# Two small products of each chunk alternate in one TensorE call, and the hand-written order of a recurrence and gated MLP kernel is rewritten

## The chip, the cores and the metric

The kernel runs on one core of one Trainium2 chip. The metric is device time in microseconds (us) of one execution. The inputs are laid out on the host before the launch; all arithmetic is on the chip. Three timed runs and one profiled run of the kernel before are at hand.

## The reference

A recurrence over 768 time steps (4 batches, 8 heads, head size 40) is followed by a gated MLP over its output. Cut to what matters:

```python
for t in range(S):                                   # S = 768, state: B x H x 40 x 40
    y[:, :, t] = einsum('bhd,bhde->bhe', r_t, state)
    Sa = einsum('bhde,bhe->bhd', state, a_t)
    state = state * w_t[:, :, None, :] - einsum('bhd,bhe->bhde', Sa, b_t)
    state = state + einsum('bhd,bhe->bhde', v_t, k_t)
x = y with the heads side by side                    # B x S x 320
h = maximum(x @ w_in, 0); u, v = halves of h         # 512 columns each
v_n = (v - mean(v)) / sqrt(var(v) + 1e-6)
gated = u * (w_spatial @ v_n + b_spatial)
out = gated @ w_out
```

## The kernel before, in words

The recurrence is worked in chunks of 64 time steps. There are 24 chunks: 12 in time for each of two pairs of batches. In a chunk the 16 heads of a pair lie as 8 units on the columns and 2 parities on the partitions (0 to 63 and 64 to 127). The recurrence inside a chunk becomes a triangular system, so that a chunk is a sequence of small fp32 products. TensorE runs each fp32 product as two instructions, so that a call with 16 products is 32 instructions in a trace.

The first phase (function `phase1`) has five kinds of calls; a call is a short function that issues one step of one chunk.

- Preparation: `prep_load` fetches the early inputs (tile `ein`), `scan1` and `scan2` are the two running products on VectorE, `at_mul` and `sl_mul` scale the inputs by them (tiles `at`, `sl`). `lprime` is the triangular block on TensorE and `lblock` masks it into tile `Lc`. Four chunks at a time are inverted on VectorE in 33 steps (`invert`, lines L636 to L663, most of the steps being the pair L652 and L656).
- Products of a chunk that don't need the state. `b_lka` (L790) multiplies the keys `sl` by `at` into a PSUM tile `bk`, and `b_lka_out` copies the two halves on ScalarE (L807) and masks them on GpSimd (L797). `b_h` (L820) multiplies the two halves of the late inputs (tile `lin`) into another `bk`, and `b_h_out` copies (L830) and masks it likewise. `b_tok` (L842), `b_l21` (L859), `b_zt` (L879) and `b_x21` (L907) are smaller ones. All of them, and `lprime`, take their PSUM from one pool with two banks, `bk`.
- The chain through the state: `c_bp` (L943), `c_bp_out` on ScalarE (L952), `c_ff` (L960), `c_ff_out` (L968), `c_xx` (L981), `c_xx_out` (L992), `c_mp` (L1005, L1011), `c_mp_out` on VectorE (L1025 or L1028 and L1029), which gives the state (tile `Mc`) of the next chunk's `c_bp`; and `c_y` (L1039), `c_y_out` (L1053), which give the chunk's output. `c_bp` and `c_xx` of a chunk are already written so that two groups alternate product by product.
- The MLP's first half on blocks of 128 steps whose chunks are done: `m_load`, `m_split`, `m_u` (L1160), `m_v` (L1114) and the normalisation `m_n1`, `m_root`, `m_n2`, `m_n3`. Their PSUM is one bank, `pv`; before the first block that bank is idle.
- `dec`: six decodings of the 64-bit input weights on VectorE, nine steps each.

Each engine takes its instructions in program order. That order is a table written out by hand: `SCHED` gives each call a place on an axis of about one unit per chunk, the calls are sorted by place (`plan.sort()`), and those below 24 are issued in exactly that order. The order on SyncE's queue, which issues nearly all DMAs, comes from the same table. Calls from 24 on and the second phase are ordered by the tile framework's scheduler. The second phase (`phase2`) is the spatial product (L423), the gate (L429) and the output projection (L478). Its weights are prepared during the first phase by `wprep` (three generators of 13 steps: one DMA, four differences L337, eight casts and differences L350 and L348) and four decodings of 9 steps. A second table, `W_PLAN`, gives a place on the same axis to each of these steps; the step is put behind the instruction that stands at that place. The first spatial product needs the weights of all three generators.

Of the kernel before, what the change touches and what calls it, by code (L numbers as in the profile page):

```python
# [8 lines left out]
F32 = mybir.dt.float32  # L9
# [25 lines left out]
    "at_mul": (-27657, -25313, -23639, -18952, -9411, 2307, 12016, 21892, 22896, 33609, 48172, 63070,  # L35
        75123, 78303, 98223, 107429, 122495, 124169, 145260, 160660,),
    "b_copy": (-29498, -29163, -16943, -7737, -5728, -5561, 7663, 7831, 17037, 17205, 30596, 31600, 39970,
# [19 lines left out]
    "b_tok": (-26987, -28828, -12759, 3813, 298, 2139, 14192, 8333, 28085, 23733, 43151, 42314, 55538,  # L57
# [3 lines left out]
    "b_tok_out": (-26150, -28493, -12591, 4483, 465, 2809, 16200, 9170, 28253, 25909, 43485, 43820, 55705,  # L61
# [3 lines left out]
    "b_w": (-24643, -20793, -16274, -25648,),  # L65
    "b_w_out": (-24309, -20626, -16106, -25480,),
# [1357 lines left out]
```

## Time and profile before

| | us |
|---|---|
| median of three runs | 670.09 (668.71 to 677.4) |
| the profiled execution, its own time | 670.43 |
| its span, first to last instruction | 668.5 |
| TensorE matmul busy | 564.6 (84%) |
| VectorE busy | 529.1 (79%) |
| ScalarE busy | 419.3 (63%) |
| GpSimd busy | 216.3 (32%) |

Busy time is the time in which an engine has at least one instruction running, so that overlapping matmuls count once. The span has three kinds of stretches, seen in the table of windows: a start, in which every engine waits at times; the chunks, in which TensorE and VectorE both work most of the time; and the second phase, in which TensorE hardly stops. An engine's idle time matters only where the next link of the chain waits for that engine.

### The profile page before, as it was taken

Reading aid. Unit: us, or ns where it says so; the run is one execution under the profiler, and the core shown is the slowest. Engines: PE = TensorE matmul, PEld = TensorE weight load, DVE = VectorE, ACT = ScalarE, POOL = GpSimd, SP = SyncE. Lnnn points to the kernel's source line nnn. Section 1 sums busy time; section 2 is a strip of 40 time slices with the busy share of each in tenths; the row PEclk is TensorE's granted clock in tenths of the full one; section 3 lists DMA queues with packets and bytes.
Section 4 is the critical chain, followed back from the end, with each engine's and each line's share of the span. In section 5 each row is a group of like instructions: output and inputs, shape, how many; then the busy total and the mean of one; then the engine's idle time right before and its main releaser. Section 6 shows DMA issues by size and latency. Waiting matters only on the chain.

```text
span 668.5 us, 27225 instructions
## 1 busy us (share of the span) xinstructions
PE 564.6 (84%) x11504; PEld 498.1 (75%) x11504; DVE 529.1 (79%) x1111; ACT 419.3 (63%) x934; POOL 216.3 (32%) x290
## 2 busy tenths in 40 slices
PE   1657778868768787997999898997998999999997
PEld 1546667656656676786888786886887899999997
DVE  7885369898999899997999679866859987776752
ACT  3344556676757788876888687795975654434422
POOL 5201122143544465522433333240424300522221
PEclk9965877899898999998999889896999999999999
DMA  8375523157466464455554553344346755444111
GB/s 191 62 146 98 120 41 93 38 133 132 80 146 141 104 122 98 106 125 126 157 128 114 146 151 107 104 116 134 102 131 195 232 179 164 138 126 139 58 50 59
DMA packets 116169, 80.79 MB, mean 121 GB/s; under 512 B 45648, under 2 KB 108368, under 8 KB 114448
## 3 DMA queue, kind: packets, MB, share of 16 engines
q1 hardware_dynamic: 115504, 77.35, 46.8%
q10 hardware_dynamic: 544, 1.72, 1.2%
q8 instruction: 90, 1.47, 1.0%
q14 instruction: 31, 0.25, 0.2%
HBM read 58.52 MB, written 20.50 MB: 118 GB/s over the span
## 4 chain that ended last, share of the span: by engine, by line
PE 48%; DVE 26%; DMA 9%; issue 6%; ACT 5%; SPq 5%; DVEq 0%; ACTq 0%
PE pg L423 12%; PE po L478 6%; DMA ein<-in_early 5%; DVE itmp L652 4%; PE pv L1114 4%; PE pv L1160 4%; PE ch L960 3%; DVE A L656 3%; PE bp L943 2%; PE bp L1039 2%; DVE sl L604 2%; DVE S L571 2%; PE ch L981 2%; DVE Et L580 2%; PE bk L842 2%
## 5 line engine op out<-in xcount | busy, mean ns | idle before, releaser
L797 POOL TENSOR_SCALAR_AFFINE_SELECT Rt<-Rt 64x256 f32<-64x256 f32 (+1 forms) x144 | 86.5, 601 | 173.1 <-ACT Rt L992 84.4
L797 POOL TENSOR_SCALAR_AFFINE_SELECT At<-At 64x512 f32<-64x512 f32 x48 | 41.7, 871 | 107.3 <-ACT At L807 105.8
L216 POOL TENSOR_TENSOR gl<-g,gh 128x384 fp32r<-128x384 f32 x32 | 33.8, 1065 | 106.7 <-ACT gh L212 106.7
L952 ACT ACTIVATE Rt<-bp 64x416 f32<-64x416 f32 x96 | 49.0, 511 | 19.6 <-PE bp L943 17.8
L652 DVE TENSOR_TENSOR itmp<-A 128x84 f32<-128x84 f32 (+12 forms) x130 | 58.1, 447 | 3.3
L992 ACT ACTIVATE Rt<-ch 64x416 f32<-64x416 f32 x96 | 49.0, 511 | 10.9 <-PE ch L981 8.9
L960 PE MATMUL ch<-Rt,At 128*64 128x104 f32 x768 | 50.1, 272 | 3.8 <-issue 3.1
L960 PEld LDWEIGHTS ch<-Rt,At 128*64 128x64 f32 x768 | 40.5, 146 | 13.8 <-issue 9.6
L656 DVE TENSOR_TENSOR A<-A,itmp 128x84 f32<-128x84 f32 (+12 forms) x130 | 45.1, 347 | 4.5
L842 PE MATMUL bk<-ident,sl 128*128 128x128 f32 x192 | 33.9, 306 | 7.1 <-DVE Lc L628 5.1
L617 PE MATMUL bk<-at,sl 64*32 64x32 f32 x1536 | 21.0, 205 | 20.9 <-DVE sl L604 14.1
L571 DVE TENSOR_TENSOR_SCAN S<-ein,ends 128x528 f32<-128x528 f32 x24 | 31.0, 1294 | 8.7 <-DMA ein<-in_early 8.7
L1039 PE MATMUL bp<-Rt,tk 128*64 128x64 f32 (+1 forms) x768 | 35.1, 243 | 1.2 <-POOL Rt L797 1.0
L1160 PE MATMUL pv<-xh,wh 128*128 128x256 f32 x123 | 26.2, 321 | 11.5 <-ACT vr L1120 7.6
L830 ACT ACTIVATE Rt<-bk 64x512 f32<-64x512 f32 x48 | 28.2, 588 | 12.1 <-PE bk L820 11.0
L820 PE MATMUL bk<-lin 64*64 64x64 f32 x768 | 30.2, 231 | 4.5 <-issue 2.3
L212 ACT ACTIVATE gh<-g 128x384 fp32r<-128x384 f32 x32 | 16.2, 519 | 27.3 <-DVE g L429 27.2
L1039 PEld LDWEIGHTS bp<-Rt,tk 128*64 128x64 f32 (+1 forms) x768 | 29.5, 152 | 4.9 <-POOL Rt L797 2.0
L617 PEld LDWEIGHTS bk<-at,sl 64*32 64x32 f32 x1536 | 17.8, 116 | 20.5 <-DVE sl L604 14.3
L943 PE MATMUL bp<-lin,Mc 64*64 64x104 f32 x384 | 26.1, 275 | 8.0 <-DVE y L1053 7.2
L807 ACT ACTIVATE At<-bk 64x512 f32<-64x512 f32 x48 | 28.2, 590 | 7.5 <-PE bk L790 6.8
L216 POOL TENSOR_TENSOR xl<-xt,xh 128x512 fp32r<-128x512 f32 x12 | 16.3, 1362 | 50.8 <-ACT xh L212 15.7
(187 smaller groups left out, 1753.4 us busy)
## 6 DMA issues: line engine op xcount, KB each, us to landing
ein<-in_early SPq DMA_DIRECT2D x40, 258.0 KB
lin<-in_late SPq DMA_DIRECT2D x48, 128.0 KB
uts<-ur SPq DMA_DIRECT2D x48, 128.0 KB
vns<-vr SPq DMA_DIRECT2D x24, 256.0 KB
raw<-vns SPq DMA_DIRECT2D x48, 128.0 KB
ut<-uts SPq DMA_DIRECT2D x48, 128.0 KB
Rt<-in_vtok SPq DMA_DIRECT2D x48, 80.0 KB
xs<-y SPq DMA_DIRECT2D x48, 80.0 KB
```

Source lines behind the costliest of these rows:

```text
L216: eng.tensor_tensor(out=lo, in0=x, in1=hi.bitcast(F32), op=ALU.subtract)
L423: nc.tensor.matmul(pg, lhsT=x[:, i], rhs=y[i][:, w], start=first and i == 0 and n == 0, stop=i == KT - 1 and n == 2, skip_group_check=True,)
L571: nc.vector.tensor_tensor_scan(out=sx[:, ::-1], data0=wseg[:, ::-1], data1=ends[:, ::-1], initial=0.0, op0=ALU.mult, op1=ALU.add,)
L652: nc.vector.tensor_tensor(out=tp, in0=A[:, k + 1:, k:k + 1].broadcast_to([P, m, k]), in1=A[:, k:k + 1, 0:k].broadcast_to([P, m, k]), op=AL ...
L656: nc.vector.tensor_tensor(out=A[:, k + 1:, 0:k], in0=A[:, k + 1:, 0:k], in1=tp, op=ALU.add)
L797: nc.gpsimd.affine_select(out=t, in_=t, pattern=[[0, k], [1, C]], base=0, channel_multiplier=-1, compare_op=ALU.is_gt, fill=0.0,)
L842: nc.tensor.transpose(pt[:, n, :], sl[:, h * NP + n].rearrange("p q c -> p (q c)"), ident)
L952: nc.scalar.activation(Rt[par][PR[par], gp, :], st["bp", g][PR[par]], AF.Copy)
L960: nc.tensor.matmul(ff[PR[1 - par], q, :], lhsT=At[par][:, n, :], rhs=Rt[par][:, n, :], start=True, stop=True,)
L992: nc.scalar.activation(Rt[par][PR[par], gp], xx[PR[1 - par ^ flip(s, g)]], AF.Copy, scale=-1.0)
L1039: nc.tensor.matmul(bp[par * 64:par * 64 + m, q, 0:C], lhsT=tk.rearrange("p n a e -> p (n a e)")[:, k:k + m], rhs=Rt[par][:, n, 0:C], start ...
L1160: nc.tensor.matmul(pu, lhsT=l, rhs=r, start=(j == 0), stop=(j == len(mm) - 1))
```

## The change

`b_lka` and `b_h` of the chunks 1 to 23 become one call, `b_lkh`. Its products alternate: two of the keys, then two of the late inputs, unit by unit. The keys' products go from the partitions of one parity to those of the other, as before; the late inputs' products now stay on their own partitions, and `b_h_out` copies across. For the chunks 1 to 10 the late inputs' result lies in the bank `pv`, which is idle there; from chunk 11 on it takes the second `bk` bank. Chunk 0 keeps its two calls.

```diff
+    def b_lkh(s):
+        Et, at, sl = st["pre", s]
+        li = lin[s % 2]
+        pk = ps_k.tile([P, NU, C], F32, name="bk")
+        if s < 11:
+            ph = ps_m.tile([P, DH], F32, name="pv").rearrange("p (n c) -> p n c", n=NU)
+        else:
+            ph = ps_k.tile([P, NU, C], F32, name="bk")
+        for n in range(NU):
+            for par in range(2):
+                nc.tensor.matmul(
+                    pk[PR[1 - par], n, :], lhsT=sl[PR[par], n, 1 - par, :], rhs=at[PR[par], n, :],
+                    start=True, stop=True,
+                )
+            for par in range(2):
+                nc.tensor.matmul(
+                    ph[PR[par], n, :], lhsT=li[PR[par], n, 0:C], rhs=li[PR[par], n, C:2 * C],
+                    start=True, stop=True,
+                )
+        st["pk", s], st["ph", s], st["hflip", s] = pk, ph, True
+
...
-            nc.scalar.activation(Rt[par][ev, :, 0:C], st["ph", s][ev], AF.Copy)
+            src = PR[par] if ("hflip", s) in st else ev
+            nc.scalar.activation(Rt[par][ev, :, 0:C], st["ph", s][src], AF.Copy)
...
-        for fn in (b_lka, b_l21, b_l21_out, b_zt, b_zt_out, b_h, b_x21, b_x21_out):
+        for fn in (b_lkh, b_l21, b_l21_out, b_zt, b_zt_out, b_x21, b_x21_out):
```

Every place below 24 in `SCHED` is new (1,601 calls before, 1,578 now), and so are most of `W_PLAN`. The end of `W_PLAN` shows the kind of edit (the pair is a place and a generator: 0 to 2 the spatial weights, 3 to 6 the output weights):

```diff
-    (23.53, 2), (23.56, 2), (23.59, 2), (23.84, 2), (23.84, 2), (23.84, 2), (23.84, 2), (23.84, 2),
-    (23.84, 2), (23.84, 2), (23.84, 2),
...
+    (23.5711, 1), (23.84, 2), (23.84, 2), (23.84, 2), (23.84, 2), (23.84, 2), (23.84, 2), (23.84, 2),
+    (23.84, 2), (23.8671, 6), (23.8681, 1), (23.8681, 1), (23.8681, 1), (23.8681, 1), (23.8836, 2),
+    (23.8836, 2), (23.8836, 2), (23.8836, 2), (23.8836, 2),
```

Three places in the order matter below. The numbers behind a tile's name tell buffers apart. Line numbers of the changed kernel are 21 higher than before from `b_lkh` on, and two or one lower ahead of it.

First, TensorE at chunk 16, before: the keys' product (16 products into one `bk` bank) between the chain's `c_bp` (bp0, bp1) and `m_v`; the late inputs' product of that chunk stands 36 rows further down.

```order
L943 MATMUL bp0_6362<-lin1_137,Mc_129 64x104 x2
L943 MATMUL bp1_6363<-lisw1_139,Mc_129 64x104 x2
L943 MATMUL bp0_6362<-lin1_137,Mc_129 64x104 x2
L943 MATMUL bp1_6363<-lisw1_139,Mc_129 64x104 x2
L943 MATMUL bp0_6362<-lin1_137,Mc_129 64x104 x2
L943 MATMUL bp1_6363<-lisw1_139,Mc_129 64x104 x2
L790 MATMUL bk_6395<-at_3787,sl_3788 64x64 x16
L1114 MATMUL pv_6424<-wh_140,xh_5778 128x512 x3
L1114 MATMUL pv_6424<-wl_141,xh_5778 128x512 x3
L1114 MATMUL pv_6424<-wh_140,xl_5779 128x512 x2
```

And in the changed kernel: a transpose `b_tok` into one `bk` bank, half of `c_y`, and the first of the 16 alternating rows, which fill two `bk` banks.

```order
L863 MATMUL bk_6303<-ident_126,sl_3891 128x128 x4
L1060 MATMUL bp1_5960<-Rt00_132,tk_5511 64x64
L1060 MATMUL bp1_5960<-Rt10_133,tk_5511 64x64
L1060 MATMUL bp1_5960<-Rt00_132,tk_5511 64x64
L1060 MATMUL bp1_5960<-Rt10_133,tk_5511 64x64
L1060 MATMUL bp1_5960<-Rt00_132,tk_5511 64x64
L1060 MATMUL bp1_5960<-Rt10_133,tk_5511 64x64
L1060 MATMUL bp1_5960<-Rt00_132,tk_5511 64x64
L1060 MATMUL bp1_5960<-Rt10_133,tk_5511 40x64
L805 MATMUL bk_6335<-at_3890,sl_3891 64x64 x2
L810 MATMUL bk_6336<-lin0_136 64x64 x2
L805 MATMUL bk_6335<-at_3890,sl_3891 64x64 x2
```

Between the last user of a `bk` bank and the call that needs both banks stands only half of `c_y`.

Second, VectorE at the end of chunk 1, before: the outputs y and the state Mc of chunk 1, then the inversion of the chunks 4 to 7 begins (A from Lc), and a scan of a later chunk follows.

```order
L1053 TENSOR_TENSOR y1_1087<-bp1_1195,Et_251 104x4x64
L1025 TENSOR_TENSOR Mc_129<-ch_1405,scn_1216 104x4x40
L1053 TENSOR_TENSOR y0_1191<-bp0_1194,Et_251 104x4x64
L636 STREAM_TRANSPOSE A_1675<-Lc_1254 128x1024
L638 MEMSET A_1675 128x32
L646 SCALAR_TENSOR_TENSOR A_1675<-A_1675 128x30
L646 SCALAR_TENSOR_TENSOR A_1675<-A_1675 128x29 x2
L571 SCALAR_TENSOR_TENSOR S_1684<-ein1_121,ends_124 128x528
L575 RECIPROCAL ends_124<-S_1684 128x8
L604 TENSOR_TENSOR sl_1683<-ein1_121,S_1684 128x1024
```

And in the changed kernel, the same rows of chunk 1 (bk into Lc, Mc, y, and the inversion's first steps).

```order
L603 TENSOR_TENSOR sl_1184<-ein0_120,S_1185 128x1024
L1046 TENSOR_TENSOR Mc_129<-ch_1392,scn_1506 104x4x40
L627 TENSOR_TENSOR Lc_1414<-bk_1531,maskl_125 128x256
L635 STREAM_TRANSPOSE A_1565<-Lc_1414 128x1024
L637 MEMSET A_1565 128x32
L645 SCALAR_TENSOR_TENSOR A_1565<-A_1565 128x30
L645 SCALAR_TENSOR_TENSOR A_1565<-A_1565 128x29 x2
L1074 TENSOR_TENSOR y1_1137<-bp1_1163,Et_251 104x4x64
L1046 TENSOR_TENSOR Mc_129<-ch_1393,scn_1506 104x4x40
L1074 TENSOR_TENSOR y0_1148<-bp0_1162,Et_251 104x4x64
L651 TENSOR_TENSOR itmp_1639<-A_1565 128x84
L655 TENSOR_TENSOR A_1565<-A_1565,itmp_1639 128x28x3
```

The inversion's first steps stand ahead of chunk 1's last Mc and outputs instead of behind them, and the scan that followed has gone further up.

Third, VectorE around the outputs y0 and y1 of the last chunk, before: the low parts of the second spatial weight (wsl1) and the differences of the third (tt) ahead of them, a normalisation, y1 and y0, and then the casts of the third weight.

```order
L1144 TENSOR_SCALAR q_9111<-q_9111,mv_9109 128x1
L348 TENSOR_TENSOR wsl1_9688<-raw_9665,wsh1_9687 128x384
L348 TENSOR_TENSOR wsl1_9688<-tt_9682,wsh1_9687 128x768 x2
L348 TENSOR_TENSOR wsl1_9688<-raw_9665,wsh1_9687 128x768
L337 TENSOR_TENSOR tt_9759<-raw_9753 128x384 x2
L337 TENSOR_TENSOR tt_9759<-raw_9753,tt_9759 128x384 x2
L1126 BN_STATS bs_9172<-vr_9167 128x6
L1128 BN_AGGR mv_9174<-bs_9172 128x2
L1130 TENSOR_SCALAR q_9176<-mv_9174 128x1
L1053 TENSOR_TENSOR y1_9042<-bp1_9059,Et_6583 104x4x64
L1053 TENSOR_TENSOR y0_9032<-bp0_9058,Et_6583 104x4x64
L350 CAST wsh2_9764<-raw_9753 128x384
```

And in the changed kernel, from y0 on.

```order
L1074 TENSOR_TENSOR y0_9018<-bp0_9044,Et_6495 104x4x64
L1147 BN_STATS bs_9198<-vr_9191 128x6
L1149 BN_AGGR mv_9200<-bs_9198 128x2
L1151 TENSOR_SCALAR q_9202<-mv_9200 128x1
L1074 TENSOR_TENSOR y1_9034<-bp1_9045,Et_6495 104x4x64
L258 TENSOR_TENSOR d_t2_9736<-d_t2_9736,woh_9661 128x320
L347 TENSOR_TENSOR wsl1_9745<-raw_9669,wsh1_9744 128x384
L347 TENSOR_TENSOR wsl1_9745<-raw_9669,wsh1_9744 128x768
L347 TENSOR_TENSOR wsl1_9745<-tt_9711,wsh1_9744 128x768 x2
L1161 RECIPROCAL q_9202<-q_9202 128x1
L259 TENSOR_TENSOR wol_9662<-d_t2_9736,d_t1_9735 128x320
L1147 BN_STATS bs_9256<-vr_9247 128x6
```

The low parts wsl1 and the differences tt stand behind the last outputs now; behind the twelve rows shown come the casts, four differences and low parts of the third weight, and then the first row of the second phase.

## Rows read from the trace of the kernel before

**Rows 1.** Busy time in four stretches: start, middle, last chunks, second phase

```profile
core 0: us, PE busy (x) PEld busy (x) DVE busy (x) ACT busy (x) POOL busy (x), PEclk, DMA share, GB/s
9.00:99.10 90.10, 59.18 (x1956) 51.08 (x1956) 61.10 (x98) 41.49 (x102) 15.77 (x29) 0.78 0.55 103
99.10:300.20 201.10, 160.95 (x4572) 134.10 (x4566) 185.68 (x362) 148.12 (x325) 85.36 (x103) 0.94 0.52 110
300.20:504.60 204.40, 188.03 (x4048) 160.68 (x4043) 160.51 (x394) 159.01 (x356) 66.30 (x99) 0.94 0.47 126
504.60:668.50 163.90, 156.46 (x948) 152.25 (x944) 116.43 (x251) 69.24 (x151) 40.82 (x38) 1.00 0.44 134
```

**Rows 2.** Timeline of TensorE at 269 us: start us, us, engine line op out<-in xcount

```profile
269.27 0.76 PE L617 MATMUL bk<-at,sl 64*32 64x32 f32 x64
269.95 1.16 PE L820 MATMUL bk<-lin 64*64 64x64 f32 x32
271.05 0.64 PE L960 MATMUL ch<-Rt,At 128*64 128x104 f32 x6
```

**Rows 3.** Timeline of TensorE at 291 us

```profile
291.76 0.94 PE L981 MATMUL ch<-ffs,xf 64*64 64x104 f32 x32
292.63 0.72 PE L1114 MATMUL pv<-wh,xh 128*128 128x512 f32 x2
```

**Rows 4.** Groups of VectorE, 99.1 to 300.2 us: busy us, mean ns of one, idle before

```profile
L652 DVE TENSOR_TENSOR itmp<-A 128x84 f32<-128x84 f32 (+12 forms) x84 | 37.8, 450 | 2.1
L656 DVE TENSOR_TENSOR A<-A,itmp 128x84 f32<-128x84 f32 (+12 forms) x84 | 28.8, 343 | 2.9
L571 DVE TENSOR_TENSOR_SCAN S<-ein,ends 128x528 f32<-128x528 f32 x12 | 16.0, 1335 | 0.5 <-DMA ein<-in_early 0.5
...
L604 DVE TENSOR_TENSOR sl<-ein,S 128x1024 f32<-128x1024 f32 x11 | 15.3, 1399 | 0.0
```

**Rows 5.** Groups over the whole span

```profile
L807 ACT ACTIVATE At<-bk 64x512 f32<-64x512 f32 x48 | 28.2, 590 | 7.5 <-PE bk L790 6.8
...
L243 DVE SCALAR_TENSOR_TENSOR d_t<-d_t,d_t 128x512 f32<-128x512 int32 (+1 forms) x10 | 6.6, 659 | 0.3
```

**Rows 6.** Waits of TensorE: us in total, times, longest us

```profile
PE bk L842 <- DVE Lc L628: 5.1, 3, 2.4
...
PE bk L820 <- DMA lin<-in_late: 2.1, 2, 1.4
```

**Rows 7.** Timeline of VectorE, 498 to 513 us

```profile
498.56 0.55 DVE L348 TENSOR_TENSOR wsl<-raw,wsh 128x384 fp32r<-128x384 f32 x1
...
501.85 1.43 DVE L337 TENSOR_TENSOR tt<-raw 128x384 f32<-128x384 f32 x2
...
504.47 0.69 DVE L1126 BATCH_NORM_STATS2 bs<-vr 128x6 f32<-128x512 f32 x1
...
505.48 0.74 DVE L1053 TENSOR_TENSOR y<-bp,Et 104x256 f32<-104x256 f32 x2
506.14 1.73 DVE L350 CAST wsh<-raw 128x384 fp32r<-128x384 f32 x2
...
508.73 0.54 DVE L348 TENSOR_TENSOR wsl<-raw,wsh 128x384 fp32r<-128x384 f32 x1
...
512.64 1.48 DVE L216 TENSOR_TENSOR la<-raw,ha 128x384 fp32r<-128x384 f32 x3
```

**Rows 8.** Timeline of TensorE, 504 to 510 us

```profile
503.99 0.69 PE L1039 MATMUL bp<-Rt,tk 128*64 128x64 f32 x16
504.61 0.96 PE L1114 MATMUL pv<-wh,xh 128*128 128x512 f32 x3
...
506.55 0.40 PE L1160 MATMUL itmp<-xh,wh 128*128 128x256 f32 x2
508.50 0.50 PE L1160 MATMUL pv<-xh,wh 128*128 128x256 f32 x2 [1.55 <-ACT vr L1120]
...
510.27 0.34 PE L423 MATMUL pg<-wsh,ha 128*128 128x384 f32 x1
```

More of the change, by code (lines that the diff above doesn't have):

```diff
@@ L144 @@
-    "m_load": (91694, 96716, 117306, 129358, 137727, 155973, 177065, 194808, 204182, 231133, 245950,
+    "at_mul": (-27040, -24410, -23587, -16024, -10927, -10762, 14395, 17683, 26727, 36099, 46622, 61585,
+        68162, 76219, 93812, 106638, 109104, 121929, 131466, 155472,),
+    "b_copy": (-29671, -28685, -17175, -12242, -4843, 4036, 6502, 20479, 19821, 26069, 30015, 30509, 40045,
[3 rows of a table added]
+    "b_h_out": (-21943, -27862, -17010, -17833, -3363, 6667, 7818, 17026, 24754, 23603, 34290, 32975,
[7 rows of a table added]
+    "b_lka_out": (-25725, -25396, -16846, -16188, -3856, -3034, 8147, 8476, 19985, 20150, 31824, 32153,
[3 rows of a table added]
@@ new lines @@
+    "b_lkh": (-28191, -19148, -4021, 7653, 19163, 30837, 45965, 50075, 58132, 70300, 83618, 99238, 103020,
+        124560, 129657, 139358, 147415, 167968, 177012, 189508, 194112, 209075, 222229,),
+    "b_tok": (-29836, -27534, -8625, 912, -2705, 13737, 14724, 10449, 28042, 24425, 37086, 39059, 56159,
[3 rows of a table added]
+    "b_tok_out": (-29507, -27369, -7803, 1076, -2541, 13902, 18012, 11435, 37250, 26562, 37414, 40210,
[3 rows of a table added]
+    "b_w": (-24903, -14051, -17504, -26711,),
+    "b_w_out": (-24738, -13886, -16682, -26218,),
[6 rows of a table added]
@@ new lines @@
+    "b_xcopy": (18506, 30180, 27878, 38401, 59941, 60105, 80001, 92004, 102198, 109433, 115845, 139194,
+        149717, 162542, 162049, 180958, 194934, 208417, 219762, 230450,),
+    "b_xt": (-20957, -12406, -2212, -25232,),
+    "b_xt_out": (-20299, -11420, -1719, -25067,),
+    "b_zt": (-13722, -5336, 3872, 18670, 28207, 40703, 44814, 60598, 68491, 79178, 89373, 106473, 114694,
+        120120, 137056, 150868, 157774, 164351, 174710, 199209, 203320, 217131, 227655, -24245,),
+    "b_zt_out": (-12078, -5172, 6174, 19328, 29358, 42840, 44978, 61092, 69971, 81645, 91510, 107460,
+        114859, 120778, 138372, 151690, 159089, 165337, 175039, 199867, 203484, 217789, 229792, -22765,),
@@ new lines @@
+    "c_bp": (-29342, -30000, -15037, -2870, 9627, 21136, 31495, 41032, 51555, 60927, 71944, 82796, 92990,
+        104829, 116667, 128013, 141002, 152512, 163200, 173723, 182602, 195592, 212363, 223380, 231930,),
+    "c_bp_out": (-28520, -29013, -14873, -11913, 748, -2377, 9955, 11764, 22287, 23109, 32811, 32646,
[3 rows of a table added]
+    "c_ff": (-26054, -28849, -12571, -11749, 2392, 1405, 11600, 12422, 22452, 23274, 35112, 34619, 42347,
[3 rows of a table added]
+    "c_ff_out": (-25889, -27698, -11584, -10433, 2556, 2063, 12093, 12586, 27056, 27549, 35277, 34784,
[3 rows of a table added]
@@ new lines @@
+    "c_mp": (-17668, -18490, -8296, -5007, 4694, 5351, 15710, 14066, 29029, 28535, 39388, 37579, 48267,
[3 rows of a table added]
+    "c_mp_out": (-15695, -15859, -7967, -4678, 4858, 9462, 18341, 18999, 29193, 31002, 39881, 37908, 49746,
[3 rows of a table added]
+    "c_xx": (-20792, -20134, -10269, 3378, 12751, 27713, 36757, 45142, 57474, 66189, 76712, 86906, 98252,
+        110419, 120614, 133932, 146264, 157609, 168461, 178491, 189179, 203649, 218118, 228148, 236040,),
+    "c_xx_out": (-18161, -18983, -8460, -10105, 4529, 5187, 15546, 12915, 28864, 28371, 38072, 36921,
[3 rows of a table added]
@@ new lines @@
+    "c_y": (-17997, -18819, -5829, -6323, 5023, 5516, 16532, 15875, 29686, 29851, 39223, 38565, 48431,
[3 rows of a table added]
+    "c_y_out": (-16517, -17339, -4514, -6158, 9298, 8969, 16697, 16368, 31331, 30673, 39552, 38730, 50568,
[3 rows of a table added]
+    "dec": (-21779, -21121, -19641, -16353, -15366, -15202, -14544, -14380, -7638, -19970, 7325, 16204,
[18 rows of a table added]
+    "lblock": (-9940, -9447, -8954, -7145, 4365, 15053, 22616, 22781, 33633, 43827, 52213, 62407, 75068,
+        82303, 98910, 107295, 118147, 123080, 136399, 159583,),
+    "lin_load": (-23094, -13557, 6996, 10613, 27384, 31988, 42183, 52048, 61256, 72273, 84440, 94963,
+        111241, 117161, 130644, 141167, 152841, 167475, 179971, 182767, 200524, 213185,),
@@ L145 @@
+    "lin_load_swapped": (-9611, 6009, 12257, 18177, 35441, 31660, 54844, 58296, 64873, 72108, 99074,
+        111570, 104993, 127355, 145935, 154321, 152677, 168133, 192796, 203977, 211705, 219269,),
+    "lprime": (-10598, -9776, -9282, -7309, 4200, 13408, 22123, 20807, 32317, 41689, 50404, 61749, 74903,
+        82138, 95785, 106966, 117983, 122258, 134590, 155636,),
+    "m_load": (90195, 93977, 102362, 117818, 142811, 158596, 174216, 185726, 204306, 229134, 245950,
         260550,),
-    "m_n1": (107262, 121323, 125340, 134212, 146767, 151119, 163506, 172545, 180413, 187778, 198156,
-        200500, 209037, 219248, 226613, 234146, 236657, 246450, 253350, 259400, 267950, 276450, 283350,
+    "m_n1": (107789, 109926, 121600, 130808, 136070, 152348, 157938, 163693, 174052, 184246, 188850,
+        196907, 201675, 211048, 225682, 234561, 237849, 246450, 253350, 259400, 267950, 276450, 283350,
@@ L185 @@
[L185 to L189 removed]
[3 rows of a table removed]
+    "open_act": (90031,),
@@ new lines @@
+    "prep_load": (-26876, -23423, -18655, -15531, 7160, -6487, 14559, 17848, 34126, 45471, 49253, 62078,
[5 rows of a table added]
+    "scn_load": (-29178, -8131, 2227, 9791, 25083, 31166, 41525, 55830, 59283, 71122, 90853, -3199, 103185,
+        117490, 132288, 140345, 152183, 161884, 175203, 186877, 204142, 217296, 226339, 194276,),
+    "scr_store": (-24081, -22930, -19806, -13393, -14215, -5665, 10284, 19656, 13079, 44649, 43498, 62900,
+        71779, 97923, 96443, 109268, 114201, 125218, 139029, 145278,),
+    "sl_mul": (-28027, -24574, -22436, -21285, -8789, -12735, 10942, 17519, 25905, 36592, 45800, 56817,
+        72601, 77534, 86249, 106309, 116832, 122094, 130150, 154814,),
```

87 lines of the change are left out of this document (16 added, 71 removed), and 169 rows, old and new, of tables (SCHED, W_PLAN).

## The prediction

> **What bounds the kernel now.** I read the table of windows first. It is cut where chunk 2's and chunk 13's first products start (99.1 and 300.2 us) and where chunk 23's last product ends (504.6) [rows 1]. The reader is to see four different stretches. At the start no engine is busy: VectorE works 61.1 of 90.1 us, TensorE 59.2 at a mean granted clock of 0.78, so that it stands for a good part at the lower of its two levels, 1.2 instead of 2.4 GHz. In the middle (chunks 2 to 12) VectorE is the fuller engine, 185.7 of 201.1 us (92%), TensorE 161.0 (80%). In the last chunks it is the other way round: TensorE 188.0 of 204.4 (92%), VectorE 160.5 (79%). In the second phase TensorE works 156.5 of 163.9. So time that leaves TensorE counts in the third stretch, time that leaves VectorE in the second, and in the fourth only what delays its start counts.
>
> Next the timeline of TensorE shows how calls with one pattern differ from calls with two. In `b_h`, whose 32 instructions go to two corners of the array in turn, the next call starts 1.10 us after it (269.95 to 271.05) [rows 2]. In `c_xx`, whose 32 instructions go to four corners in turn and stream 104 columns instead of 64, it starts after 0.87 us (291.76 to 292.63) [rows 3].
>
> **The fused call.** Four instructions of 104 columns take 0.87 / 8 = 0.109 us there, so four of 64 columns take 0.067, by columns alone. The fused call has 64 instructions, 16 sets of four: 1.07 us. The other way to see it: `b_h` is 16 sets of two in 1.10 us, and two more corners are filled beside each set. I take 1.10 us for what were two calls of 1.10. This saves 1.10 us of TensorE for each of 23 chunks, 25.3 us in all. Bounds for the fused call: below, 0.68 us, the pitch of `lprime`, which is also 64 instructions (269.27 to 269.95, 32 columns) [rows 2]; above, 2.20 us, if four corners don't run beside each other at all. ScalarE's copies and GpSimd's masks keep their count and shape; that `b_h_out` now reads the other half of the partitions I cost at nothing, since its copies keep their size, 512 columns; no row here sets such a copy beside a straight one, and the bounds of the new waits, below, take it in.
>
> A rule speaks against this. The Trainium skill ("TensorE: Matmul & The Clock Gate", section on "Wait — 56ns, not 53.3ns?") says that two matmuls never start closer than about 25 ns, however few columns they stream. By it the fused call would take 64 x 25 ns = 1.6 us and save 0.6 instead of 1.10 per chunk, 14 us in all. The row of `lprime` contradicts it: 64 instructions in 0.68 us are 11 ns each [rows 2].
>
> **Middle, 99 to 300 us.** I counted the calls of both tables between the same two products. VectorE's share loses 11 inversion steps (a pair of 0.450 and 0.343 us, 8.7 us), one chunk's two scans and its `sl` (1.335 twice, as the second scan has the same shape, and 1.399: 4.1 us) and two decoding operations (0.66 each) [rows 4, 5]; it gains a normalisation and a copy, 1.5 us by the rows of the end (0.69 and little ones) [rows 7]. Sum -12.6 us. All of it stands in the start now. There VectorE is idle 29 of 90 us [rows 1], and TensorE's ping-pong with ScalarE sets the pace, so I take its cost there as 0. Bounds: 0 to +12.6, if it comes ahead of what TensorE waits for; the order shows chunk 1's last Mc behind the inversion's first steps. Lower: the start itself may lose two or three us, as one fused call replaces two for chunks 1 to 3. The waits in the middle (15.4 us) I leave as they are.
>
> **Last chunks, 300 to 504.6 us.** 19 calls of the two kinds become 10: 19 x 1.10 - 10 x 1.10 = 9.9 us. Two `m_u` fewer fall into the stretch, 1.1 us each (by the two that take 506.55 to 510.27, less the wait of 1.55) [rows 8]. Sum -12.1 us; bounds -2 (nothing runs side by side, or VectorE follows as the limit) and -13 (the idle 8% shrinks with the work).
>
> **The join with the second phase.** The weights' operations are in number the same, but more of them stand behind the last outputs. Before, from y0 and y1 (505.48) to the first low part of the second phase (512.64 and on) VectorE takes 7.6 us [rows 7]. Now the chain behind y0 is: two outputs 0.66, two normalisation heads 1.7, two products of a decoding 1.3, wsl1 3.3 (498.56 to 501.85), the casts 2.6 (506.14 to 508.73), the differences 2.6 (501.85 to 504.47), the third low parts 3.2 (508.73 to 512.64 without the normalisation's 0.69), small normalisation rows some 1.5, the low part 0.5: 17.4 us. TensorE has other work there: half of `c_y` 0.62, three `m_v` of 1.94 (504.61 to 506.55), three `m_u` of 1.1 and two spatial products, 10.0 us in all [rows 8]. It would then stand 7.4 us, against the 1.55 that it stands now. Cost: about +5, between 0 and +9. The DMA of the third weight moves late too, but some 10 us of VectorE's work stand between its buffer's last reader and its first use, so I cost it at nothing.
>
> **New waits.** From chunk 11 on the fused call needs both `bk` banks, and each stays taken until two copies of 0.59 us are done [rows 5]. By the order, chunk 16's call has half a `c_y` (0.62) behind `b_tok`, chunks 11 and 13 give the next user of a bank only 0.8 and 1.1 us, and chunk 11's call comes right behind `lprime`, whose reader sits in VectorE's queue; such a wait took 1.7 us in the mean (5.1 us in 3) [rows 6]. On SyncE's queue chunk 2's `vtok` load and chunk 4's `lin` load now stand close ahead of their users; a late `lin` has cost TensorE up to 1.4 us a time [rows 6]. I take +5 in all. What is queued behind a waiting fused call is all of TensorE, above all the chain's `c_bp`. Bounds 0 and 31: 13 calls x 4 copies x 0.59 with no cover.
>
> **Sum,** against the profiled run's own 670.4 (span 668.5, and 1.9 around it; the median of the runs is 670.1): 670.4 - 12.6 - 12.1 + 5 + 5 = 655.7 us.
>
> **Rivals.** First, the early work is not hidden: the start grows by what the middle loses, 655.7 + 12.6 = 668.3 us. For it: VectorE takes in order, and chunk 1's Mc stands behind the inversion. Against: 29 idle us. Second, everything fits better: no new waits, no gap at the join, and the waits in both stretches shrink with the work (12.6 / 0.92 and 12.1 / 0.92): 670.4 - 13.7 - 13.2 = 643.5 us. For it: every call has a new place, and the waits are many and short. Against: the row of wsl1 behind y0. Third, the one on the slower side: the two-bank call. It holds both banks until four copies are done, and ScalarE may have four other copies ahead of them; the price per call lies between 2.4 us (the four alone) and 4.4 (four more of about 0.5), 3.4 in the middle. 13 calls cost 44 us, in place of my 5: 655.7 - 5 + 44 = 695 us. It decides from about 1.5 us per call (20 / 13), where the gain is gone, and from 2.5 on it shows as slower. Against: between most of these calls and the next user of a bank stand 2 to 5 us of other products. The Trainium skill ("TensorEngine Tiling (Array Packing)", section on the PSUM bottleneck) says likewise that packing speeds up the array but not the emptying of PSUM. Fourth, the four corners don't run beside each other, as by the rule above or worse: 655.7 + 9.9 = 665.6 us.
>
> **How the numbers follow.** Forecast 0.46, first rival 0.16, second 0.22, third 0.13, fourth 0.03. Two per cent, 13.4 us, is about what a measurement of this kernel can tell from no change; 656.7 and 683.5 are the lines. The forecast lies just below the first of them, as its costs of 5 and 5 could each be 3 off; I give 0.27 of its 0.46 to faster. With the second rival that is 0.49. Same is 0.19, the first and the fourth rival, and a third of the two-bank case at a small price: 0.42. Slower is 0.09. The range 638 to 678 takes in the second rival, the first and the fourth, and leaves out most of the two-bank case and the last few per cent below.
>
> **What would show it.** Right: the fused lines' 64 instructions lie within about 1.1 us; chunk 2 starts near 99 us, chunk 13 near 288, chunk 23's last product ends near 485; TensorE has a gap of 5 to 7 us ahead of the third weight's first spatial product. Wrong: chunk 2 starts 10 us later (first rival); waits of the fused call on ScalarE's copies of more than 10 us in all, or of the next `bk` users (third); a fused call of over 1.6 us at the full clock (fourth); a mean clock in the middle well under 0.94, which would mean that sparser products have brought TensorE to its lower level more often.

## The result, and the profile after

The changed kernel takes 642.5 us in the median (639.9 to 647.0, four runs) against 669.4 us of the kernel before beside it: a ratio of 0.964, with a 95% interval of 0.954 to 0.974. The profiled execution took 643.6 us (span 641.8) for 670.4 (span 668.5) before, 26.8 us less.

The table of windows of the changed kernel, cut at the same landmarks as [rows 1]: chunk 2's first product, chunk 13's first product, chunk 23's last product, the end. The columns are those of [rows 1].

```profile
core 0: us, PE busy (x) PEld busy (x) DVE busy (x) ACT busy (x) POOL busy (x), PEclk, DMA share, GB/s
9.00:97.90 88.90, 58.38 (x1944) 50.12 (x1945) 67.63 (x108) 41.45 (x103) 19.27 (x31) 0.79 0.59 113
97.90:289.30 191.40, 157.59 (x4579) 129.08 (x4578) 177.72 (x349) 152.19 (x330) 83.01 (x104) 0.91 0.54 113
289.30:472.40 183.10, 170.52 (x4045) 145.00 (x4044) 152.94 (x386) 157.28 (x349) 67.24 (x97) 0.98 0.50 134
472.40:641.80 169.40, 158.50 (x944) 154.57 (x944) 124.72 (x260) 70.59 (x152) 42.74 (x38) 0.98 0.43 135
```

Against [rows 1] the reader is to see: the start 1.2 us shorter though VectorE works 6.5 us more in it; the middle 9.7 shorter, with 8.0 us less VectorE work; the last chunks 21.3 shorter, with TensorE 17.5 us less busy, VectorE 7.6, and the mean granted clock up from 0.94 to 0.98; the second phase with the join 5.5 longer. The sum is -26.7 us. The clock does not rise everywhere: in the middle it falls from 0.94 to 0.91, the direction that the prediction had named as a sign of being wrong, and in the second phase from 1.00 to 0.98.

One profile of a stretch is not exact to a few us. Six of the profiles here and below have the changed order in the start and in the middle, two of them with the fused call as two runs: their start took 88.6 to 92.0 us and their middle 191.4 to 196.2. A difference of 3 us in one stretch of one profile shows nothing by itself.

The fused call of one chunk, in the timeline of TensorE (start us, us, engine line op out<-in xcount), and the call behind it:

```profile
307.11 0.27 PE L805 MATMUL bk<-at,sl 64*64 64x64 f32 x2
307.13 0.27 PE L810 MATMUL bk<-lin 64*64 64x64 f32 x2
...
308.05 0.23 PE L810 MATMUL bk<-lin 64*64 64x64 f32 x2
308.20 0.50 PE L1032 MATMUL ch<-tk,Rt 128*40 128x40 f32 x14
```

The 64 instructions take 1.09 us up to the next call, where one of the two old calls took 1.10 [rows 2]. That holds for ten of the 23 fused calls (1.00 to 1.09 us); the others take longer, most of them with a wait or a stretch at the lower clock inside.

Two views of the join. First VectorE's timeline behind the last chunk's second output: the weights' operations stand there in a row, as predicted.

```profile
473.65 0.41 DVE L1074 TENSOR_TENSOR y<-bp,Et 104x256 f32<-104x256 f32 x1
473.98 1.13 DVE L258 TENSOR_TENSOR d_t<-d_t,woh 128x320 f32<-128x320 f32 x1
475.03 1.94 DVE L347 TENSOR_TENSOR wsl<-raw,wsh 128x384 fp32r<-128x384 f32 x2
476.90 1.81 DVE L347 TENSOR_TENSOR wsl<-tt,wsh 128x768 fp32r<-128x768 f32 x2
```

Then TensorE's timeline; in brackets is the idle time before a row and what ended it.

```profile
482.00 0.97 PE L1135 MATMUL pv<-wh,xh 128*128 128x512 f32 x3 [1.53 <-ACT ur L1187]
...
487.12 0.69 PE L422 MATMUL pg<-wsh,ha 128*128 128x384 f32 x1 [3.00 <-ACT ha L210]
...
489.35 0.69 PE L422 MATMUL pg<-wsh,la 128*128 128x384 f32 x1 [1.22 <-DVE q L1163]
```

TensorE stands 5.75 us in three pieces. The longest ends with `ha`, which is made from the `raw<-vns` load; SyncE issued that load only at 481.0, behind the outputs' stores and the next block's loads. The first spatial product comes 14.7 us after the last product of chunk 23, where it came 5.7 us after it before (504.6 to 510.27 [rows 8]).

### The profile page after: what moved, and what is told of

Read it like the earlier page. It is cut to its first block, busy times and chain, and to the rows that moved or that the text cites. A ratio compares the mean times of both kernels' runs of the same rounds, so it can differ in the third digit from the quotient of the medians.

```text
span 641.8 us, 27233 instructions
## 1 busy us (share of the span) xinstructions
PE 545.0 (85%) x11504; PEld 478.8 (75%) x11504; DVE 528.1 (82%) x1111; ACT 423.0 (66%) x934; POOL 220.3 (34%) x290
## 4 chain that ended last, share of the span: by engine, by line
PE 43%; DVE 28%; DMA 10%; ACT 7%; SPq 5%; issue 5%; POOL 0%; DVEq 0%; ACTq 0%; POOLq 0%
PE pg L422 14%; PE po L477 7%; DMA ein<-in_early 5%; DVE itmp L651 3%; PE pv L1181 3%; PE pv L1135 3%; DVE S L570 3%; DVE Et L579 3%; PE ch L981 3%; DVE sl L603 3%; DVE A L655 2%; PE bp L964 2%; SPq L1108 2%; DMA scr<-sc 2%; PE ch L1002 2%
## 5 line engine op out<-in xcount | busy, mean ns | idle before, releaser
L214 POOL TENSOR_TENSOR gl<-g,gh 128x384 fp32r<-128x384 f32 x32 | 35.1, 1103 | 102.5 <-ACT gh L210 102.5
L817 POOL TENSOR_SCALAR_AFFINE_SELECT At<-At 64x512 f32<-64x512 f32 x48 | 40.3, 839 | 58.0 <-ACT At L827 56.3
L981 PE MATMUL ch<-Rt,At 128*64 128x104 f32 x768 | 54.4, 284 | 4.6 <-issue 3.1
L981 PEld LDWEIGHTS ch<-Rt,At 128*64 128x64 f32 x768 | 43.7, 154 | 12.2 <-issue 5.3
L570 DVE TENSOR_TENSOR_SCAN S<-ein,ends 128x528 f32<-128x528 f32 x24 | 33.0, 1374 | 8.4 <-DMA ein<-in_early 5.6
L210 ACT ACTIVATE gh<-g 128x384 fp32r<-128x384 f32 x32 | 16.4, 521 | 28.8 <-DVE g L428 25.8
L214 POOL TENSOR_TENSOR xl<-xt,xh 128x512 fp32r<-128x512 f32 x12 | 20.4, 1696 | 42.8 <-ACT xh L210 33.8
L1002 PE MATMUL ch<-ffs,xf 64*64 64x104 f32 x768 | 28.6, 273 | 6.5 <-ACT ffs L989 4.1
L603 DVE TENSOR_TENSOR sl<-ein,S 128x1024 f32<-128x1024 f32 x24 | 30.7, 1282 | 3.8 <-PE bk L863 3.7
L827 ACT ACTIVATE At<-bk 64x512 f32<-64x512 f32 x48 | 28.3, 590 | 7.7 <-PE bk L805 6.7
L805 PE MATMUL bk<-at,sl 64*64 64x64 f32 x736 | 30.3, 233 | 3.0 <-issue 1.7
L579 DVE TENSOR_TENSOR_SCAN Et<-ein,ends 128x528 f32<-128x528 f32 x24 | 32.3, 1345 | 0.2
```

The source lines that it names most:

```text
L214: eng.tensor_tensor(out=lo, in0=x, in1=hi.bitcast(F32), op=ALU.subtract)
L570: nc.vector.tensor_tensor_scan(out=sx[:, ::-1], data0=wseg[:, ::-1], data1=ends[:, ::-1], initial=0.0, op0=ALU.mult, op1=ALU.add,)
L579: nc.vector.tensor_tensor_scan(out=Et, data0=wseg, data1=ends, initial=0.0, op0=ALU.mult, op1=ALU.add,)
L603: eng.tensor_tensor(out=sl[:, ns], in0=oth[:, ns, 1:], in1=sv[:, ns, 2:C + 2].unsqueeze(2).broadcast_to([P, k, 2, C]), op=ALU.mult,)
L817: nc.gpsimd.affine_select(out=t, in_=t, pattern=[[0, k], [1, C]], base=0, channel_multiplier=-1, compare_op=ALU.is_gt, fill=0.0,)
L981: nc.tensor.matmul(ff[PR[1 - par], q, :], lhsT=At[par][:, n, :], rhs=Rt[par][:, n, :], start=True, stop=True,)
```

## The experiments

All times are medians, beside runs of the kernel before on the same chip. The kernel before took 669 to 676 us from chip to chip, so the ratios are compared, and stretches are read at the landmarks above.

**The alternation alone.** In the changed kernel, with all places and banks as they are, the fused call becomes two runs of 32:

```diff
             for par in range(2):
                 nc.tensor.matmul(pk[PR[1 - par], n, :], ...)
+        for n in range(NU):
             for par in range(2):
                 nc.tensor.matmul(ph[PR[par], n, :], ...)
```

> The changed kernel with every call in its new place and with the same banks; only the 64 instructions of the fused call stand as two runs, first the 32 of the keys, then the 32 of the late inputs, each to two corners in turn. Theory (fusion is worth its TensorE time where TensorE bounds, and the new places are worth the rest): each call takes 2.1 us and more instead of 1.0; ten such calls stand after chunk 13's first product, so the last stretch grows by about 11 us, the middle, which VectorE bounds, by 2 to 5, the start by 0 to 3: 655 to 660 us. Rival 1 (nearly all of the gain is the alternation): 23 x 1.1 = 25 us more, about 668. Rival 2 (all of it is the new places): no more than 3 us, about 645. The clock in the last stretch: if it stays at 0.96 or above with the two runs, the higher clock there comes from the places and not from the alternation.

Measured: 649.4 us, ratio 0.9625 (0.957 to 0.968), on a chip where the kernel before took 675.8. That ratio is the changed kernel's own, so it was run again beside the changed kernel on one chip:

> The changed kernel as it is, on the same chip as the next three, so that they can be set against it there. Theory and rivals alike: 3.0 to 4.5% under the kernel before (0.955 to 0.97).

> The changed kernel with the fused call as two runs of 32, once more, now beside the changed kernel on one chip. In the first profile of it two runs back to back took 1.84 us (310.65 to 312.49) against 1.09 for the fused call, 0.75 us x 23 = 17 us of TensorE, and the span was 7 us longer. Theory (about 40 to 50% of what TensorE saves comes through): 5 to 9 us above the changed kernel. Rival 1 (all comes through): 17 us. Rival 2 (none, the 7 us were the chip): within 3 us.

Measured: the changed kernel 650.3 us, ratio 0.963 (0.958 to 0.968); the two runs 650.9 us, ratio 0.965 (0.960 to 0.970). The timeline of TensorE of the first such kernel: the keys' run, the late inputs' run, and the next call (a few rows in which the two runs overlap are left out).

```profile
310.65 0.97 PE L805 MATMUL bk<-at,sl 64*64 64x64 f32 x26
...
311.58 0.98 PE L811 MATMUL bk<-lin 64*64 64x64 f32 x27
312.49 0.86 PE L1033 MATMUL ch<-tk,Rt 128*40 128x40 f32 x15
```

The windows of its middle and last chunks:

```profile
97.60:292.90 195.30, 165.27 (x4586) 137.91 (x4582) 176.51 (x349) 151.31 (x330) 82.87 (x104) 0.90 0.54 111
292.90:479.40 186.50, 176.19 (x4045) 151.31 (x4044) 150.73 (x386) 156.90 (x349) 65.56 (x97) 0.98 0.49 132
```

Those of the second such profile, and below them the last chunks of the changed kernel on that chip:

```profile
98.90:290.80 191.90, 163.98 (x4584) 136.93 (x4580) 180.05 (x349) 151.14 (x330) 83.10 (x104) 0.91 0.54 115
290.80:479.10 188.30, 177.73 (x4045) 153.12 (x4044) 150.37 (x386) 156.71 (x349) 65.14 (x97) 0.97 0.47 128
```

```profile
291.50:472.90 181.40, 169.45 (x4045) 143.99 (x4044) 151.40 (x386) 156.87 (x349) 65.66 (x97) 0.99 0.51 135
```

Two runs back to back take 1.84 us, not 2.20, so the alternation saves 0.75 us per call, some 17 us of TensorE's work in 23 calls. Little of that reaches the time. The two medians are 0.5 us apart with some 4 us of uncertainty on each, and the first run has the changed kernel's own ratio: rival 2 of both expectations (no more than 3 us) fits them best, and my 5 to 9 us stands at their edge. The profiled spans are 5.7 and 7 us longer, but executions of one kernel differ by as much: the profiled one of the changed kernel on that chip, 644.7 us, is the fastest of six with a median of 650.3. In the last chunks the two runs take 186.5 and 188.3 us where the changed kernel takes 183.1 and 181.4; but the kernel with VectorE's work put back, below, has the alternating calls in the same order there and takes 187.8. That leaves 3 us in the mean, for 7.5 us of TensorE's work in ten calls. In the middle (195.3 and 191.9 for 191.4 and 192.6) and in the start nothing shows. So the alternation itself is worth between nothing and 7 us. Rival 1 (25, or 17, us) is out; my own 11 us for the last chunks was at least twice too high. The clock of 0.97 to 0.98 in the last chunks stays with the two runs, and so does the 0.90 to 0.91 in the middle: both come from the places.

**The fused call without the new places.** The kernel before with its own tables; 18 chunks get one `b_lkh` entry at the later of the two old places, or a little behind it, with the four copies right behind. The other five keep their two calls.

> The kernel before with its own tables of places; only the two products of chunks 1 to 9, 12, 13, 15 and 18 to 23 are one fused call, at the later of the two old places or a little behind it, with its four copies right behind it. Theory: seven of these 18 calls stand after chunk 13's first product and save 1.1 us each, 7.7, the start saves 1 to 3, the middle 0 to 2, and the copies that come later cost 0 to 5: 658 to 666 us. Rival 1 (nearly all is the alternation): 18 x 1.1 = 20 us, about 650. Rival 2 (all is the new places): 668 to 672 us, or slower by the copies that come late.

Measured: 703.7 us, ratio 1.043 (1.037 to 1.048): slower by 28 us. Of the three expectations only rival 2 allowed for this, and not for its size. Its windows, the middle and the last chunks, and its largest waits of TensorE in the middle (us in total, times, longest; L1141 is `c_mp`, L1128 `c_xx_out`):

```profile
100.60:333.60 233.00, 172.60 (x4569) 141.48 (x4567) 186.12 (x368) 149.84 (x324) 76.42 (x102) 0.82 0.45 96
333.60:535.50 201.90, 180.34 (x4047) 153.48 (x4042) 158.45 (x390) 160.72 (x357) 71.53 (x101) 0.96 0.47 126
```

```profile
PE ch L1141 <- ACT Rt L1128: 12.1, 9, 3.6
PE ch L1096 <- ACT Rt L1088: 5.6, 4, 3.6
```

One wait of the last chunks (L925 is the fused call's half of the late inputs, L1004 the copy of `b_l21`):

```profile
PE bk L925 <- ACT l L1004: 6.1, 1, 6.1
```

The middle loses 32 us: TensorE's idle time there goes from 40 to 60, and the clock falls to 0.82. The largest waits are on ScalarE's copies of the chain (12.1 us for those of `c_xx`, 5.5 before), which stand in one queue with those of the fused calls. In that stretch the fused calls up to chunk 9 put their second result into the idle bank `pv`; only chunk 12's holds both `bk` banks. So the 32 us are not the third rival's two banks; late copies are the likely cause, which was not tried by itself. In the last chunks, where seven fused calls hold both banks, one waits 6.1 us for a bank, the third rival's case, and the stretch is 2.5 us shorter all the same, no more than such a stretch varies. A fused call of chunks 10, 11, 14, 16 and 17 in the old places was not tried.

**The weights' table alone, both ways.** The changed kernel with the old `W_PLAN`, and the kernel before with the new one (its last five entries at 23.88, just inside the old calls' range).

> The changed kernel with the table of the weights' operations of the kernel before; the calls keep their new places. Theory: the stretch from the last product to the first spatial product shrinks from 14.8 us to 8 to 10, as about 10 us of VectorE's work go back ahead of the last outputs; the last chunks grow by 3 to 6 us, since VectorE is idle there for 30 of 183 us but in pieces: 639 to 647 us in all. Rival A (the work ahead hides whole): about 637. Rival B (the weights' new places are what took TensorE's long waits out of the last chunks): these waits come back, with 5 to 10 us of half clock behind them, 650 us or more.

> The kernel before with the changed kernel's table of the weights' operations, and nothing else. Theory: the wait of VectorE on the load of the output weights (4.8 us at 447 us) goes or moves, the last chunks get 3 to 8 us shorter, the join gets 4 to 6 us longer: 665 to 673 us. Rival B (the weights' places made the last chunks faster): 8 us or more less, 661 or below. Rival C (they are costs alone): 673 to 676.

Measured: 655.1 us, ratio 0.969 (0.963 to 0.975), and 668.1 us, ratio 0.989 (0.983 to 0.994). The windows of the last chunks and of the join with the second phase, first of the changed kernel with the old table, then of the kernel before with the new one:

```profile
294.10:487.60 193.50, 174.74 (x4045) 148.85 (x4044) 158.61 (x396) 157.58 (x350) 66.77 (x97) 0.96 0.49 131
487.60:652.30 164.70, 156.78 (x944) 152.25 (x944) 117.02 (x250) 69.73 (x151) 41.44 (x38) 1.00 0.43 132
```

```profile
299.20:495.90 196.70, 181.13 (x4047) 155.60 (x4043) 153.47 (x387) 158.56 (x355) 65.28 (x99) 0.97 0.47 125
495.90:667.10 171.20, 160.61 (x944) 154.71 (x944) 123.94 (x257) 70.48 (x152) 43.77 (x38) 0.98 0.43 135
```

Both directions agree on the stretches, one profile each. The new table takes some 8 to 10 us out of the last chunks (204.4 to 196.7, and 193.5 to 183.1) and gives 5 to 7 back behind them (163.9 to 171.2, and 164.7 to 169.4). Six to seven us less VectorE work stand in the last chunks. In the medians the table is worth 7.7 us in the kernel before (668.1 for 675.8) and about 4 in the changed kernel (0.969 for 0.963), the second inside the intervals. I had expected the last chunks to grow by only 3 to 6 us with the old table; where the kernel before takes 670 us the ratios stand for 649 and 662 us in all, next to rival B's 650 and 661 and outside my own ranges.

How the table does it is less clear than rival B says. With the new table alone TensorE still waits in the place of the kernel before's long wait at 455 us (the next experiment but one):

```profile
PE pv L1161 <- ACT ur L1167: 3.5, 1, 3.5
```

And with the old table in the changed kernel that wait does not come back; others do, of 3.1 and 2.8 us. What goes with the table in both directions is the time at the lower clock in the last chunks: 23.8 us in the kernel before and 10.2 with the new table alone, 17.0 in the changed kernel with the old table and 3.4 to 10.2 in the profiles with the new one.

**VectorE's early work put back.** In the changed kernel chunk 9's scans and products and inv1's first seven steps stand behind chunk 2's first product again (twelve entries of `SCHED`, from -1.31 to -0.35 to just behind -0.287, and chunk 11's `prep_load` with them).

> The changed kernel with VectorE's early work put back: chunk 9's scans and products (1.335 twice, 1.4 and about 0.75, 4.8 us) and inv1's first seven steps (seven times 0.79, 5.5 us) stand behind chunk 2's first product again instead of ahead of it; the load of chunk 11's early inputs moves with them. Theory (VectorE sets the middle's pace, the start hides the work): chunk 2 starts where it did (97 to 98 us) and chunk 13 starts 7 to 10 us later, 6 to 10 us more in all. Rival (the middle's pace is set elsewhere, by waits between engines): chunk 13 within 3 us of the changed kernel's, no more than 3 us in all. Second rival (the early work was in the way at the start): chunk 2 starts 4 us or more earlier.

Measured: 657.8 us, ratio 0.977 (0.971 to 0.982), 7.5 us above the changed kernel on the same chip. The start and the middle:

```profile
9.00:95.40 86.40, 59.21 (x1943) 50.20 (x1947) 60.92 (x98) 41.19 (x102) 20.87 (x31) 0.74 0.60 111
95.40:300.30 204.90, 161.86 (x4589) 133.37 (x4579) 183.24 (x360) 151.92 (x331) 82.34 (x104) 0.88 0.52 110
```

And its last chunks, whose order is the changed kernel's:

```profile
300.30:488.10 187.80, 172.04 (x4045) 146.22 (x4044) 151.00 (x386) 156.63 (x349) 65.32 (x97) 0.97 0.49 129
```

The middle grows to 204.9 us, clear of the 191.4 to 196.2 of the six profiles with the new order, and the start shrinks by 2.5 to 3.5, so that chunk 2 starts 2 us earlier than I had expected; the second rival asked for 4. The theory holds in sign and in the total; the first rival (3 us) is out. The start is the shortest of all the profiles, so that hiding the work may cost something there, but one profile does not tell. At a clock of 0.88 instead of 0.91 the middle lost 9 to 13 us for the 10.3 us of work that came back.

**One wait in the kernel before.** Seven entries of the old `W_PLAN`: the first decoding of the output weights moves from 21.15 to 21.42 to 21.31 to 21.43, behind chunk 20's last Mc. What it is about, in the kernel before: VectorE waits for a load, ScalarE for VectorE, TensorE for ScalarE. (Rows of the timelines of the three engines.)

```profile
452.17 0.33 DVE L226 TENSOR_SCALAR d_t<-raw 128x320 int32<-128x320 int32 x1 [4.82 <-DMA raw<-in_wout]
...
454.11 0.81 ACT L1149 ACTIVATE vr<-vr,q 128x512 f32<-128x512 f32 x1 [3.66 <-DVE q L1144]
...
455.24 0.62 PE L1160 MATMUL pv<-xh,wh 128*128 128x256 f32 x3 [3.09 <-ACT ur L1166]
```

It is one of four waits of TensorE of some 3 us in the last chunks (us in total, times, longest; the others end at 312.5, 379.9 and 417.1 us). The one at 379.9, of 2.78 us, is of another kind: ScalarE's `vr` waits 4.45 us there for the store of an earlier `vr`.

```profile
PE pv L1160 <- ACT vr L1120: 6.1, 2, 3.3
PE bp L943 <- DVE y L1053: 5.0, 4, 3.1
PE pv L1160 <- ACT ur L1166: 3.1, 1, 3.1
```

Behind each of the four stands a stretch at the lower of TensorE's two levels, 1.2 GHz (a granted clock of 0.50), in which TensorE is full or nearly full:

```profile
312.70:316.10 3.40, 3.40 (x75) 3.11 (x75) 1.74 (x6) 2.86 (x6) 0.00 (x0) 0.50 0.58 150
381.00:387.80 6.80, 6.80 (x93) 6.12 (x94) 6.26 (x17) 4.98 (x13) 1.85 (x2) 0.50 0.74 205
418.50:421.90 3.40, 3.40 (x10) 2.31 (x8) 3.34 (x7) 2.53 (x5) 0.00 (x0) 0.50 0.15 40
456.00:466.30 10.30, 9.35 (x98) 7.26 (x99) 6.61 (x18) 5.40 (x11) 1.45 (x2) 0.50 0.55 156
```

> The kernel before with seven entries of its table of the weights' operations moved: the first decoding of the output weights begins behind chunk 20's last Mc (21.31 to 21.43 for 21.15 to 21.42) instead of ahead of a y and a normalisation. There VectorE waited 4.8 us for the load (447.1 to 452.2), the normalisation behind it came late, so did ScalarE's copy out of the one bank, TensorE waited 3.1 us (to 455.24), and its clock stood at the lower level from 456.0 to 466.3. Theory (a short wait costs itself and the lower clock behind it): the wait of 3.1 us shrinks to 1 or less, the 10 us at the lower clock go or shrink to 3.4, chunks 20 and 21 take 5 to 8 us less together (42.7 before), and the whole 4 to 8 us less. Rival 1 (the clock falls there anyway): 2 to 3 us less. Rival 2 (something else is late next): within 1.5 us.

Measured: 666.2 us, ratio 0.996 (0.990 to 1.002): no difference that the runs can tell. In its profile (span 664.6, 3.9 less) TensorE's row in that place and the stretch at the lower level are:

```profile
453.10 0.62 PE L1149 MATMUL pv<-xh,wh 128*128 128x256 f32 x3 [1.20 <-ACT ur L1155]
```

```profile
455.40:458.80 3.40, 3.40 (x63) 2.89 (x56) 2.98 (x7) 1.97 (x5) 0.63 (x1) 0.50 0.61 132
```

The wait goes from 3.1 to 1.2 us, the lower level behind it from 10.3 to 3.4, and chunks 20 and 21 take 38.0 us instead of 42.7. That is the place as the theory had it. But the lower level changed as much where nothing was moved: of the other three stretches, 13.6 us together, 6.8 are left in this profile, behind waits of 2.2 and 3.1 us, and none stands behind one of 2.8. So one profile does not show that the shorter wait brought the clock back. The size of the whole is inside the runs' uncertainty, and neither rival (2 to 3 us, or within 1.5) is out.

**The join mended.** In the changed kernel five entries of `W_PLAN`, the second spatial weight's low part and the last product of a decoding, move from 23.867 and 23.868 to 23.671 and 23.672, ahead of the last outputs (`W_EAGER` from 23.6 to 23.7, so that they go to the front there).

> The changed kernel with five of the weights' operations that stand behind the last outputs (the four of the second spatial weight's low part and the last product of a decoding, 1.94 + 1.81 + 1.13 + 0.47 = 5.4 us) moved ahead of them, into VectorE's gap of 3.9 us at 467 us; the loads of the second phase's first operand then come earlier in SyncE's queue. Theory: the first spatial product comes 3 to 6 us earlier and the half clock of 7 us behind the gap shrinks; 3 to 7 us less in all. Rival (the loads of the first operand wait for the stores of the first phase, not for VectorE): no more than 2 us. Second rival: the last outputs come later by as much as the join wins, 0.

Measured: 646.1 us, ratio 0.9595 (0.955 to 0.965), 4.3 us under the changed kernel on the same chip. The window from the last product to the first spatial product, and that product's row:

```profile
479.40:487.60 8.20, 7.18 (x41) 6.11 (x42) 6.36 (x21) 3.99 (x9) 2.02 (x2) 1.00 0.86 269
```

```profile
487.57 0.34 PE L485 MATMUL pg<-wsh,ha 128*128 128x384 f32 x1
```

The first spatial product comes 8.2 us after the last product instead of 14.7, at the upper clock, where the changed kernel has this behind its wait:

```profile
487.10:493.90 6.80, 5.56 (x19) 5.06 (x20) 6.09 (x16) 4.11 (x9) 0.00 (x0) 0.50 0.58 188
```

SyncE issues the load for the first operand 0.7 us behind the last product there, ahead of the outputs' stores, where it stood 8.6 us behind it. By the place of the first spatial product the first rival is out; the medians alone, 4.3 us with some 4 us of uncertainty on each, would not tell it from the theory. This is the fastest version beside the changed kernel on that chip, by a margin (0.9595 against 0.963) that the intervals do not separate.

## Why the prediction was right, and where it was off

The direction and the range held; the forecast of 655.7 us was 13 too high. By its steps, in the profiled execution:

- **Start, 0 forecast: -1.2.** The early work is hidden, for the most part at least; the first rival is out, by the start's own length and by the kernel with the work put back.
- **Middle, -12.6 forecast: -9.7.** The mechanism is shown: VectorE sets the pace there, and what leaves it leaves most of its time with it (7.5 us in the medians for 10.3 us of work). The sign of a lower clock in the middle did appear, 0.91 for 0.94; with the alternation taken out it stays, so the new places make it and not the alternation. One more detail was wrong. Of the eleven inversion steps only seven stand in the start now; four, of inv4, went into the last chunks.
- **The fused call, 1.10 us forecast: 1.09.** Four corners do run beside each other, 17 ns per instruction, and the fourth rival is out. But I set it against 2.20 for the two old calls. As neighbours they take 1.84 in the kernel with two runs, so only 0.75 of the 1.1 us come from the alternation.
- **Last chunks, -12.1 forecast with bounds of -2 and -13: -21.3.** This is the step that failed. I took 9.9 us for the fused calls and 2.2 for two `m_u`, and left the clock of the stretch as it was and its waits to one bound. TensorE's busy time falls by 17.5 us there and its idle time by 3.8. The forecast's 12.1 us leave 5.4 of the busy time, and the time at 1.2 GHz falls from 23.8 to 6.8 us, which can be worth 8.5 (an estimate: half of the 17.0, as TensorE is nearly full in it). So what was put at nothing is the clock, and to a smaller part the waits. The experiments say where it comes from: 8 to 10 us of the stretch go with the weights' table, which I had booked at the join alone, as a cost, and the clock goes with it; the alternation has 3 us in the profiles and nothing that the medians show. Which waits the table takes out is open. One is shown in a row, a load of the weights that VectorE waits 4.8 us for ahead of the normalisation; the other long ones have other causes, and one profile with that load moved does not settle what the clock does behind it. What the other new places do in this stretch was not separated.
- **Join, +5 forecast: +5.5.** TensorE stands 5.75 us where I had 5 to 7, but the size came out right by luck. What ended the longest wait was a load late in SyncE's queue, not a low part on VectorE, and 6.8 us at the lower clock stand behind it, which I did not have. Moving VectorE's work ahead cleared all of it, and the load moved ahead with it; which of the two counts was not separated.
- **New waits, +5 forecast: none in sum.** TensorE's idle time falls in the middle from 40.2 to 33.8 us and in the last chunks from 16.4 to 12.6. But the waits that I had listed are there: those for late inputs, and those of the next users of a bank for the copies of a fused call, some 4 us in all for 1 before (us in total, times, longest; L827 and L851 are these copies):

```profile
PE pv L810 <- DMA lin<-in_late: 3.7, 2, 3.4
PE bp L964 <- DMA lisw<-in_late: 3.7, 1, 3.7
...
PE bk L810 <- issue: 3.5, 1, 3.5
...
PE bk L863 <- ACT At L827: 1.8, 3, 1.1
...
PE bk L880 <- ACT Rt L851: 1.1, 1, 1.1
```

That is under the 10 us that were to show the third rival, both banks held. In the kernel with the old places one fused call waited 6.1 us for a bank, so this depends on the places. The second rival's 643.5 us is the time that came, but by another sum: it had the join at nothing and both stretches gaining 13 us.

In the medians the whole is worth some 25 us. VectorE's early work accounts for 7.5 of them, the weights' table for 4 to 8, the alternation for next to nothing that the runs can tell. The rest, some 10 to 13 us, belongs to the other new places and was not separated.

## What to carry to other kernels

Work of an engine that is only 79% busy can still cost time where it stands: moving 6 to 7 us of VectorE's work out of the last chunks took 8 to 10 us out of that stretch and put 5 to 7 behind it. So ask of such a move what it gains where the work leaves, and not only what it costs where it goes. When a fused operation comes with a new order, run the new order with the operation unfused: here that kernel could not be told from the fused one in the medians. A fusion that puts several copies in one place may need new places for them; in the one old arrangement that was tried it cost 4%.

## What the runs showed of the hardware

A call of 32 instructions on two corners takes 1.10 us between calls of other tile shapes [rows 2]. Two such calls as neighbours take 1.84 us on different corners (the two runs, 310.65 to 312.49), and 64 instructions on four corners in turn 1.09. In the kernel before, both old calls go to the same two corners, and the one `b_h` that has a `b_lka` right behind it takes 2.02 with it:

```profile
396.70 1.15 PE L820 MATMUL bk<-lin 64*64 64x64 f32 x32
...
398.72 0.62 PE L1160 MATMUL pv<-xh,wh 128*128 128x256 f32 x3
```

How much of this is the change of shape and how much the corners was not tried by itself.

In the last chunks of the kernel before, four waits of TensorE of 2.8 to 3.3 us went with 3.4, 6.8, 3.4 and 10.3 us at 1.2 GHz, and the 3.0 us at the changed kernel's join with 6.8. So a wait ahead of a full stretch can cost more than itself, and its length does not tell how much: of the same places in another profile one of 2.8 us had none behind it, and one of 1.2 us had 3.4.
